# Local attention and a two-level mixture of experts: the gathered rows turned by DMA instead of on TensorE, and layer 1 in four PSUM tiles of their own

## The chip, the cores and the metric

The kernel runs on one core of a Trainium2 chip. The metric is the device time of one execution in microseconds. Before the change it is 672.78 us, the median of 3 runs (669.76, 672.78 and 676.31).

## What is computed

Attention over 8 batches, 8 heads, 576 positions and 64 channels; the first four heads look back over a window of 32 positions, the others over 32 positions four apart. Its output, 4608 rows of 512, goes through a mixture of experts: each row picks one of 4 groups and one of the 4 experts in it, and gets that expert's two-layer network, weighted by both probabilities.

```python
scores = np.where(masks[None, :, :, :], scale * np.matmul(q, k.transpose(0, 1, 3, 2)), -1000000000.0)
attn = softmax(scores)                      # max, exp, sum + 1e-09
x = np.matmul(attn, v)                      # as 4608 rows of 512
g_idx = np.argmax(x @ w_group, axis=1)      # g_w: softmax at g_idx
e_idx = np.argmax(xg @ w_expert[g], axis=1) # e_w: softmax at e_idx
h = np.maximum(xg[mask_e] @ w1[g, e], 0.0)  # 512 -> 1024
out[tok_idx] = (g_w * e_w)[:, None] * (h @ w2[g, e])   # 1024 -> 512
```

## The kernel before

The first part (the loop at L875) is the attention, tile by tile, with the routing of finished rows woven in. The attention's rows are stored to DRAM (`xd`, L350). Its product with v goes to PSUM tiles `o` in the pool psA (L303).

The second part, from about 255 us on, runs the experts in an order by size. `PIECES` (L42) holds 16 pieces, one for each expert, of 152 to 368 rows; 256-row and 128-row parts of the two largest experts are done earlier (`early`, L863) while the attention ends. For piece i, `begin(i)` (L1030) selects the row numbers on DVE, lets POOL gather the rows from DRAM (`fetch_rows`, L688: two indirect DMAs of half a row for each tile of up to 128 rows, into `xr`), and makes the tiles `xh` and `xl`, which hold the rows turned, channels on partitions, as the high and the low half in fp16. All arithmetic of the two layers is done with such pairs: high x high, low x high, high x low, three matmuls for each product.

`spread` (L713) turns the rows. For each tile of rows PE transposes four blocks of 128 x 128 fp32 into the PSUM tile `pt` (L721), ACT copies `pt` to `xh` in fp16 (L722), and DVE subtracts for `xl` (L723).

`layer1` (L736) makes the 1024 hidden channels in 8 groups of 128, numbered 0 to 7 here: 12 matmuls into one PSUM tile of 512 columns (L743), then ACT's Relu to `hh` (L750) and DVE's `hl` (L751). The PSUM tile comes from `new_a` (L729): in turn one half of the tile `second`, which lies in psA's two banks, and a tile `a` of the pool psS, which has two.

`layer2` (L759) takes the row tiles one by one: 24 matmuls each into `y` (L802; 8 hidden groups, each with hh, hl, hh), ACT's scaled copy to `yr` (L776), and POOL's scatter to the output (L763). A last tile with at most 64 rows is packed 2 or 4 times side by side; its row numbers and weights are turned by small matmuls `rp` after group 3 of layer 1 (L664 to L669: `entq` on DVE, `csq` on ACT). In the middle and at the end of each row tile `layer2` calls `between`, and this is where the next piece's rows are spread (L1071).

The weights come as 8 chunks of 512 KB per expert, issued by SP (L611) into 7 buffers. Each chunk is split by ACT into the high half (L625: wa1h, wb2h and so on) and by DVE into the low half (L622); DVE's split frees the buffer, and the next fetch is issued after it. The main loop (L1076) spreads these splits over the steps of the piece: four or five in layer 1, the rest in layer 2. `overflow` (L955), small DVE steps for rows beyond an expert's share, fills steps that have none.

The order on every engine is the order of the program from L1057 on (`manual_schedule`); an engine stops at the first instruction whose input is not there. A DMA on SP stops SP in the same way.

Of the kernel before, what the change touches and what calls it, by code (L numbers as in the profile page):

```python
# [8 lines left out]
F32 = mybir.dt.float32  # L9
F16 = mybir.dt.float16  # L10
# [3 lines left out]
ALU = mybir.AluOpType  # L14
AX = mybir.AxisListType
PSUM = bass.MemoryType.PSUM

P = 128
B, H, S, D = 8, 8, 576, 64
NTOK = B * S  # L20
DM = 512
# [21 lines left out]
CMAX = max(n for _, _, n in PIECES)  # L43
# [21 lines left out]
def moe_attention_kernel(ctx, tc, q, k, v, cmask, wgate, wpack, out):  # L65
    nc = tc.nc
    pool = lambda name, bufs=1, **kw: ctx.enter_context(tc.tile_pool(name=name, bufs=bufs, **kw))
    cp = pool("cp")
    dram = pool("dram", space=bass.MemoryType.DRAM)
    psS = pool("psS", 2, space=PSUM)  # L70
    psT = pool("psT", 2, space=PSUM)
    psA = pool("psA", 1, space=PSUM)
    psX = pool("psX", 1, space=PSUM)
    psR = pool("psR", 1, space=PSUM)

# [19 lines left out]

    att = ExitStack()
    apool = lambda name, bufs=1, **kw: att.enter_context(tc.tile_pool(name=name, bufs=bufs, **kw))
    vp = apool("vp", NV)
    qp = apool("qp", NQ)
    kr = apool("kp").tile([P, 2, 2 * NK, 8, 32], F32, name="kr")  # L100
# [121 lines left out]
    def run(gens, n=1):  # L222
        got = None
        for _ in range(n):
            while gens:
                try:
                    got = next(gens[0])
                    break
                except StopIteration:
                    gens.pop(0)  # L230
            else:
                return None
        return got
# [454 lines left out]
    def fetch_rows(xr, ent, t, known=NTOK + 1):  # L688
        for h in range(2):
            nc.gpsimd.indirect_dma_start(  # L690
                out=xr[:, 256 * h : 256 * h + 256],
                out_offset=None,
                in_=xd[0:known].rearrange("n (h c) -> (n h) c", h=2),
                in_offset=bass.IndirectOffsetOnAxis(ap=ent[:, 1 + h, t : t + 1], axis=0),
                bounds_check=2 * known - 1,
                oob_is_err=False,
            )

    def tiles(cap):
        return [(t, min(P, cap - t * P)) for t in range((cap + P - 1) // P)]  # L700

    def gather(ent, cap):
        xrs = []
        for t, n in tiles(cap):
            xr = rows.tile([P, 512], F32, name="xr", bufs=4)
            fetch_rows(xr, ent, t)
            xrs.append(xr)
        return xrs

    def new_x(pl, cap=CMAX):  # L710
        return pl.tile([P, 4, cap], F16, name="xh"), pl.tile([P, 4, cap], F16, name="xl")

    def spread(xs, xrs, cap, sel=None):  # L713
        xh, xl = xs
        for t, n in tiles(cap):
            if sel is not None and t not in sel:
                continue
            xr = xrs[t]
            pt = psT.tile([P, 4, P], F32, name="pt", tag="t")
            for c in range(4):  # L720
                nc.tensor.transpose(pt[:, c, 0:n], xr[0:n, c * P : c * P + P], id32[0:n, 0:n])  # L721
            nc.scalar.copy(xh[:, :, t * P : t * P + n], pt[:, :, 0:n])  # L722
            nc.vector.tensor_tensor(  # L723
                xl[:, :, t * P : t * P + n], pt[:, :, 0:n], xh[:, :, t * P : t * P + n], ALU.subtract
            )

    more_a = []

    def new_a():  # L729
        if more_a:  # L730
            more_a.append(more_a.pop(0))
            if more_a[0] is not None:
                return more_a[0]
        return psS.tile([P, 512], F32, name="a", tag="s")

    def layer1(w, xs, cap, new_h):  # L736
        xh, xl = xs
        hh, hl = hs[:] = new_h()
        for f in range(8):
            a = new_a()  # L740
            mm = [(ww, xx, c) for c in range(4) for ww, xx in ((w[0], xh), (w[0], xl), (w[1], xh))]
            for i, (ww, xx, c) in enumerate(mm):
                nc.tensor.matmul(  # L743
                    a[:, 0:cap],
                    ww[:, c * FF + f * P : c * FF + f * P + P],
                    xx[:, c, 0:cap],
                    start=(i == 0),
                    stop=(i == len(mm) - 1),
                )
            nc.scalar.activation(hh[:, f, 0:cap], a[:, 0:cap], AF.Relu)  # L750
            nc.vector.scalar_tensor_tensor(  # L751
                hl[:, f, 0:cap], a[:, 0:cap], 0.0, hh[:, f, 0:cap], ALU.max, ALU.subtract
            )
            yield
# [120 lines left out]
    for s in range(NT + 3):  # L875
# [12 lines left out]
        if start:  # L888
            n = start.pop()
# [23 lines left out]
        if s == NT - 1:  # L913
            room = fe.tile([P, 48 * P], F16, name="room")
            cut = lambda a, c: room[:, a * P : (a + c) * P].rearrange("p (c n) -> p c n", c=c)
            for i in range(2):
                xs, hs_ = (cut(24 * i, 4), cut(24 * i + 4, 4)), (cut(24 * i + 8, 8), cut(24 * i + 16, 8))
# [15 lines left out]
    fx = pool("fx", 2, reuse_waits="tile")  # L933
    fh = pool("fh", 2, reuse_waits="tile")
    rows = pool("rows", 2, reuse_waits="tile")
# [3 lines left out]
    def new_h():  # L939
        return fh.tile([P, 8, CMAX], F16, name="hh"), fh.tile([P, 8, CMAX], F16, name="hl")  # L940

    second = psA.tile([P, 2, 512], F32, name="second", tag="o")
    more_a[:] = [None, second[:, 0], None, second[:, 1]]
    spare = xT[NBP - 1].rearrange("p c b i -> p (c b i)")
    taken = [0]

# [79 lines left out]
    nt = lambda c: (c + P - 1) // P  # L1026

    pieces = PIECES

    def begin(i):  # L1030
        r, off, cap = pieces[i]
        ent, cs = new_slots()
        three = select(ent, cs, top[:, r] if r < NEARLY else perm[:, r], off // P, nt(cap))
        tq = note_tail(cs, three, cap)
        return ent, cs, gather(ent, cap), new_x(fx), tq

    cur = []

    def first(k):
        if 0 < k <= nt(pieces[0][2]):  # L1040
            spread(cur[3], cur[2], pieces[0][2], (k - 1,))

    def ready():
        cur[:] = begin(0)
# [18 lines left out]
    for i, (r, off, cap) in enumerate(pieces):  # L1063
        more = i + 1 < len(pieces)
        if more:
            nxt = begin(i + 1)
            ncap = pieces[i + 1][2]
            nc.gpsimd.drain()
        nsel = nt(cap)

        def between(k):  # L1071
            m, d = nt(ncap), 2 * nsel - 2
            if more and k < d:
                spread(nxt[3], nxt[2], ncap, range(m * k // d, m * (k + 1) // d))

        for k, _ in enumerate(ffn(wsets[r % 2], cur[3], cur[0], cur[1], cap, new_h, between, cur[4])):  # L1076
            k0, steps = (0, 8) if k < 8 else (8, 2 * nsel)
            if k == 0:
                todo = ahead
            elif k == 8:  # L1080
                ahead = split(r + 2, wsets[r % 2]) if r + 2 < NE else []
                todo, ahead = ahead[: NW // 2], ahead[NW // 2 :]
            if k == k0:
                chunks = len(todo)
            if (k - k0 + 1) * chunks // steps > (k - k0) * chunks // steps:
                todo.pop(0)()
            elif r > NEARLY:
                run(bgq)
        if more:
            cur = nxt  # L1090
# [3 lines left out]
    with tc.For_i(0, nov, 1) as i:  # L1094
# [13 lines left out]
        ent, cs = new_slots()  # L1108
        unpack(ent, cs, three.unsqueeze(2))
        xs = new_x(fx)  # L1110
        xr = gather(ent, P)
# [73 lines left out]
```

## Time and profile before

| | |
|---|---|
| median of 3 runs | 672.78 us |
| the profiled execution | 663.49 us, span 661.7 us, mean granted clock 0.959 |
| PE, DVE, ACT, POOL busy | 588.1, 405.4, 331.6, 249.2 us |
| hardware DMA queue | 105.31 MB |
| gathers and scatters (software DMA queue) | 20.98 MB |

The profile is of one execution. Busy time of PE is the time in which at least one matmul is under way; matmuls overlap, so a count times a mean is more than the busy time. PEld is the load of the stationary operand, which runs beside matmuls. An idle time is put down to the engine and line that ended it. The chain of work that ended last goes back from the last instruction, at each step to what released it. Times in the timeline count from the span's start.

### The profile page before, as it was taken

To read this page: it belongs to the slowest core of one execution; us is meant where nothing else is said; L and a number is where in the kernel's file an instruction comes from. 1 tells how busy PE (TensorE), PEld (TensorE's weight loads), DVE (VectorE), ACT (ScalarE), POOL (GpSimd) and SP (SyncE) were. 2 spreads that over 40 slices of the span, in tenths; PEclk is the share of its full clock that TensorE was granted. 3 is DMA by queue.
4 is the path that set the end of the run, shared out by engine and by line. 5 is a ranking of instruction groups with operands and counts; after the bars stand their busy time and mean duration, and the time that the engine had idled before them with its cause. 6 is when DMAs were issued, how large, how long until landed. Compare 5 with 4: busy or idle time off the path is not lost.

```text
span 661.7 us, 18758 instructions
## 1 busy us (share of the span) xinstructions
PE 588.1 (89%) x7636; PEld 407.9 (62%) x7636; DVE 405.4 (61%) x849; ACT 331.6 (50%) x662; POOL 249.2 (38%) x304
## 2 busy tenths in 40 slices
PE   5898799878577999879989899898999999999896
PEld 4666576556464677655556566555576577667764
DVE  6765875887834672457485777554556567575720
ACT  2455565665532643456354455454557556556521
POOL 5874554539040171415142333414154134213311
PEclk9899989898796999979999999999999999999999
DMA  7887867796551026557565656656585677678300
GB/s 260 277 280 232 258 199 224 244 333 225 164 183 37 25 72 238 192 162 245 162 189 194 181 181 207 195 163 208 157 267 193 193 259 226 236 234 266 94 27 28
DMA packets 47916, 127.53 MB, mean 193 GB/s; under 512 B 7224, under 2 KB 8126, under 8 KB 47826
## 3 DMA queue, kind: packets, MB, share of 16 engines
q1 hardware_dynamic: 40466, 105.31, 50.0%
q0 software_dynamic: 7360, 20.98, 9.3%
q8 instruction: 62, 1.02, 0.6%
q14 instruction: 28, 0.23, 0.1%
HBM read 107.38 MB, written 19.24 MB: 191 GB/s over the span
## 4 chain that ended last, share of the span: by engine, by line
PE 57%; DVE 5%; issue 5%; ACT 3%; another core or an unknown queue 1%; POOL 0%; POOLq 0%; ACTq 0%
PE y L802 29%; PE second L743 12%; PE a L743 11%; PE pt L721 3%; DVE hl L751 1%; ACT hh L750 1%; PE lg_ps L389 1%; ACT wa1h L625 1%; ACT wa2h L625 1%; DVE wb1l L622 1%; PE lt_ps L378 0%; DVE wa1l L622 0%; DVE mv L492 0%; ACT wb2h L625 0%
## 5 line engine op out<-in xcount | busy, mean ns | idle before, releaser
L690 POOL DMA_INDIRECT xr<-xd,sent x80 | 96.5, 1206 | 33.2 <-issue 22.2
L763 POOL DMA_INDIRECT out<-yr,sent x30 | 30.0, 1001 | 204.6 <-ACT yr L776 180.8
L802 PEld LDWEIGHTS <-hh 128*128 128x128 f16 (+10 forms) x960 | 67.8, 99 | 59.8 <-issue 4.8
L743 PEld LDWEIGHTS <-wa1h 128*128 128x128 f16 x640 | 59.3, 98 | 25.7 <-issue 14.2
L723 DVE TENSOR_TENSOR xl<-pt,xh 128x512 f16<-128x512 f32 (+10 forms) x42 | 24.8, 595 | 77.7 <-ACT xh L722 69.0
L743 PEld LDWEIGHTS <-wb1h 128*128 128x128 f16 x576 | 55.9, 100 | 24.0 <-issue 13.2
L776 ACT ACTIVATE yr<-y,cs 128x512 f32<-128x512 f32 (+3 forms) x30 | 20.6, 688 | 91.7 <-PE y L802 67.4
L751 DVE SCALAR_TENSOR_TENSOR hl<-second,hh 128x256 f16<-128x256 f32 (+11 forms) x68 | 29.0, 427 | 55.6 <-ACT hh L750 41.4
L802 PE MATMUL y<-wb2h,hh 128*128 128x512 f16 (+6 forms) x272 | 60.6, 307 | 0.5 <-issue 0.5
L802 PE MATMUL y<-wb2h,hl 128*128 128x512 f16 (+6 forms) x272 | 60.4, 305 | 0.3
L802 PE MATMUL y<-wb2l,hh 128*128 128x512 f16 (+6 forms) x272 | 60.2, 305 | 0.5 <-issue 0.5
L802 PE MATMUL y<-wa2h,hl 128*128 128x512 f16 (+7 forms) x208 | 56.8, 330 | 0.1
L802 PE MATMUL y<-wa2h,hh 128*128 128x512 f16 (+7 forms) x208 | 56.9, 331 | 0.0
L127 POOL TENSOR_SCALAR vs<-vt 32x520 f32<-32x520 f32 x72 | 47.9, 665 | 23.8 <-DMA vt<-v 13.0
L802 PE MATMUL y<-wa2l,hh 128*128 128x512 f16 (+7 forms) x208 | 56.7, 330 | 0.0
L131 POOL TENSOR_SCALAR vs<-vt 32x520 f32<-32x520 f32 x64 | 41.9, 654 | 35.9 <-PE o L309 32.7
L802 PEld LDWEIGHTS <-hl 128*128 128x128 f16 (+10 forms) x480 | 35.0, 100 | 26.3 <-issue 1.2
L743 PE MATMUL second<-xh,wb1h 128*128 128x256 f16 (+6 forms) x144 | 39.6, 277 | 12.1 <-DVE hl L751 11.0
L750 ACT ACTIVATE hh<-a 128x256 f16<-128x256 f32 (+11 forms) x68 | 26.3, 387 | 42.9 <-PE a L743 22.0
L751 DVE SCALAR_TENSOR_TENSOR hl<-a,hh 128x256 f16<-128x256 f32 (+11 forms) x68 | 28.9, 425 | 30.1 <-ACT hh L750 19.2
L274 PE MATMUL s<-kr,qb 128*32 128x128 f32 x1152 | 43.3, 294 | 4.5 <-DMA kr<-k 2.2
L274 PEld LDWEIGHTS s<-kr,qb 128*32 128x32 f32 x1152 | 32.5, 117 | 18.0 <-issue 13.8
(201 smaller groups left out, 1552.5 us busy)
## 6 DMA issues: line engine op xcount, KB each, us to landing
w<-wpack SPq DMA_DIRECT2D x128, 512.0 KB
vt<-v SPq DMA_DIRECT2D x36, 260.0 KB
qb<-q SPq DMA_DIRECT2D x36, 256.0 KB
xd<-x SPq DMA_DIRECT2D x72, 128.0 KB
kr<-k SPq DMA_DIRECT2D x34, 256.0 KB
xr<-xd,sent POOLq DMA_INDIRECT x80
kr<-k SPq DMA_DIRECT2D x4, 128.0 KB
out<-yr,sent POOLq DMA_INDIRECT x30
```

Of the source, the lines that this page charges most:

```text
L127: nc.gpsimd.tensor_scalar(vs[n][even], vt[n][even], 1.0, 1.0, ALU.mult, ALU.mult)
L131: nc.gpsimd.tensor_scalar(vs[n][odd], vt[n - 1][odd], 1.0, 1.0, ALU.mult, ALU.mult)
L274: nc.tensor.matmul(s[32 * j : 32 * j + 32, c].rearrange("p w k -> p (w k)"), qv[:, (sl * 2 + a) * 32 : (sl * 2 + a) * 32 + 32], kr[:, :, k ...
L690: nc.gpsimd.indirect_dma_start(out=xr[:, 256 * h : 256 * h + 256], out_offset=None, in_=xd[0:known].rearrange("n (h c) -> (n h) c", h=2), ...
L721: nc.tensor.transpose(pt[:, c, 0:n], xr[0:n, c * P : c * P + P], id32[0:n, 0:n])
L723: nc.vector.tensor_tensor(xl[:, :, t * P : t * P + n], pt[:, :, 0:n], xh[:, :, t * P : t * P + n], ALU.subtract)
L743: nc.tensor.matmul(a[:, 0:cap], ww[:, c * FF + f * P : c * FF + f * P + P], xx[:, c, 0:cap], start=(i == 0), stop=(i == len(mm) - 1),)
L750: nc.scalar.activation(hh[:, f, 0:cap], a[:, 0:cap], AF.Relu)
L751: nc.vector.scalar_tensor_tensor(hl[:, f, 0:cap], a[:, 0:cap], 0.0, hh[:, f, 0:cap], ALU.max, ALU.subtract)
L763: ins = nc.gpsimd.indirect_dma_start(out=out.rearrange("n (g c) -> (n g) c", g=g), out_offset=bass.IndirectOffsetOnAxis(ap=at, axis=0), in ...
L776: nc.scalar.activation(yr[0:n, :], yp[0:n, :], AF.Copy, scale=cs[0:n, t : t + 1])
L802: nc.tensor.matmul(yp[P // g * j : P // g * j + n, 0 : DM // g], h[:, f, t * P : t * P + n], ww[:, f * DM + DM // g * j : f * DM + DM // g ...
```

## The change

The rows are turned without PE. For each gathered tile, ACT copies the 128 x 512 fp32 rows to fp16 into the left half of a tile `both`, DVE writes the rest, rows minus that copy, into the right half, and SP issues one DMA transpose of `both` (up to 128 rows x 1024) into the piece's tile `xx` (128 partitions x 8 blocks x rows), of which `xh` is the first four blocks and `xl` the others. The number of rows turned is rounded up to 16. One tile is turned for each step of the generator `turning`; the steps are taken after groups 4 and 6 of layer 1 and then at layer 2's calls of `between`. `spread` remains for the early pieces and the overflow. There are 3 buffers for `xr` and not 4.

In layer 1 the tile `second` goes; psA's banks are given back after the attention and a pool psB with two tiles takes their place, so that the 8 groups go in turn to four tiles of one bank each.

```diff
-    psA = pool("psA", 1, space=PSUM)
...
+    psA = apool("psA", 1, space=PSUM)
...
     def gather(ent, cap):
...
-            xr = rows.tile([P, 512], F32, name="xr", bufs=4)
+            xr = rows.tile([P, 512], F32, name="xr", bufs=3)
...
-    def new_x(pl, cap=CMAX):
-        return pl.tile([P, 4, cap], F16, name="xh"), pl.tile([P, 4, cap], F16, name="xl")
+    def new_x(pl):
+        xx = pl.tile([P, 8, CMAX], F16, name="xx")
+        return xx[:, 0:4], xx[:, 4:8], xx
+
+    def turning(xs, xrs, cap):
+        for t, n in tiles(cap):
+            both = rows.tile([P, 2 * DM], F16, name="both", bufs=3)
+            nc.scalar.copy(both[:, 0:DM], xrs[t])
+            nc.vector.tensor_tensor(both[:, DM : 2 * DM], xrs[t], both[:, 0:DM], ALU.subtract)
+            n = (n + 15) // 16 * 16
+            nc.sync.dma_start(xs[2][:, :, t * P : t * P + n], both[0:n], transpose=True)
+            yield
...
-    more_a = []
+    more_a = [psS]
 
     def new_a():
-        if more_a:
-            more_a.append(more_a.pop(0))
-            if more_a[0] is not None:
-                return more_a[0]
-        return psS.tile([P, 512], F32, name="a", tag="s")
+        more_a.append(more_a.pop(0))
+        return more_a[0].tile([P, 512], F32, name="a", tag="s")
...
-    second = psA.tile([P, 2, 512], F32, name="second", tag="o")
-    more_a[:] = [None, second[:, 0], None, second[:, 1]]
+    more_a[:] = [psS, pool("psB", 2, space=PSUM, reuse_waits="tile")]
...
-        return ent, cs, gather(ent, cap), new_x(fx), tq
+        xrs, xs = gather(ent, cap), new_x(fx)
+        return ent, cs, xrs, xs, tq, [turning(xs, xrs, cap)]
...
     def first(k):
-        if 0 < k <= nt(pieces[0][2]):
-            spread(cur[3], cur[2], pieces[0][2], (k - 1,))
+        run(cur[5])
...
         def between(k):
-            m, d = nt(ncap), 2 * nsel - 2
-            if more and k < d:
-                spread(nxt[3], nxt[2], ncap, range(m * k // d, m * (k + 1) // d))
+            if more:
+                run(nxt[5])
...
+            if k in (4, 6):
+                between(k)
```

Three places in the piece of 288 rows show how the instructions stand. Line numbers of the rows after the change are those of the changed file (L750 is the matmul of layer 1 there, L757 `hh`, L717 and L718 the two halves of `both`, L720 the DMA transpose).

First, PE in layer 1, at a group that waits for DVE. Before, this is the third group, number 2:

```order
L743 LDWEIGHTS wb1l
L743 MATMUL a<-xh,wb1l 128x288
L743 LDWEIGHTS wb1h
L743 MATMUL second<-xh,wb1h 128x288 [waits DVE_49]
L743 LDWEIGHTS wb1h
L743 MATMUL second<-xl,wb1h 128x288
```

And with the change the fifth, number 4, right behind the small matmuls `rp` of the tail:

```order
L666 MATMUL rp<-tq,id_73 32x2 [waits PE_49]
L666 MATMUL rp<-tq,id_73 32x2 x3
L750 LDWEIGHTS wb1h
L750 MATMUL a<-xx,wb1h 128x288 [waits DVE_49]
L750 LDWEIGHTS wb1h
L750 MATMUL a<-xx,wb1h 128x288
```

Groups 2, 4 and 6 waited for DVE before; now groups 4 to 7 do.

Second, ACT in the same layer 1, from the second pair of groups on (`wa2h` is the split of a weight chunk for a later piece). Before:

```order
L625 ACTIVATE wa2h<-w_6807 128x1024
L750 ACTIVATE hh<-second 128x288
L750 ACTIVATE hh<-a 128x288
L669 COPY csq<-rp 128x1
L625 ACTIVATE wa2h<-w_6840 128x1024
L750 ACTIVATE hh<-second 128x288
L625 ACTIVATE wa2h<-w_6859 128x1024
L750 ACTIVATE hh<-a 128x288
L750 ACTIVATE hh<-second 128x288
L625 ACTIVATE wa2h<-w_6932 128x1024
L750 ACTIVATE hh<-a 128x288
L776 ACTIVATE yr<-y,cs 128x512
```

With the change:

```order
L625 ACTIVATE wa2h<-w_6784 128x1024
L757 ACTIVATE hh<-a 128x288 x2
L669 COPY csq<-rp 128x1
L625 ACTIVATE wa2h<-w_6822 128x1024
L757 ACTIVATE hh<-a 128x288
L717 CAST both<-xr 128x512
L625 ACTIVATE wa2h<-w_6841 128x1024
L757 ACTIVATE hh<-a 128x288 x2
L717 CAST both<-xr 128x512
L625 ACTIVATE wa2h<-w_6904 128x1024
L757 ACTIVATE hh<-a 128x288
L717 CAST both<-xr 128x512
```

The three copies of gathered rows stand behind groups 4, 6 and 7; before, the three copies `xh` stood among layer 2's `yr`. DVE's subtracts stand at the same places on DVE.

Third, SP over the same stretch, where the rows before were weight fetches alone (the ISA row sets the address of a fetch):

```order
L611 DMA w_6761<-wpack 128x1024
L720 DMA_TRANSPOSE xx<-both 128x8x128
L611 ISA
L611 DMA w_6784<-wpack 128x1024
L720 DMA_TRANSPOSE xx<-both 128x8x128
L611 ISA
L611 DMA w_6822<-wpack 128x1024
L611 ISA
L611 DMA w_6841<-wpack 128x1024
L720 DMA_TRANSPOSE xx<-both 128x8x32
L611 ISA
L611 DMA w_6904<-wpack 128x1024
```

Three DMA transposes have come in between the fetches of the piece; each waits for DVE's subtract, and the fetches below it wait behind it.

More of the change, by code (lines that the diff above doesn't have):

```diff
@@ L708, in gather @@
         return xrs
-    def new_x(pl, cap=CMAX):
-        return pl.tile([P, 4, cap], F16, name="xh"), pl.tile([P, 4, cap], F16, name="xl")
+    def new_x(pl):
[9 more added lines that the diff above has]
+            yield
     def spread(xs, xrs, cap, sel=None):
-        xh, xl = xs
+        xh, xl = xs[0:2]
         for t, n in tiles(cap):
@@ L725, in spread @@
             )
-    more_a = []
+    more_a = [psS]
     def new_a():
-        if more_a:
-            more_a.append(more_a.pop(0))
-            if more_a[0] is not None:
-                return more_a[0]
-        return psS.tile([P, 512], F32, name="a", tag="s")
+        more_a.append(more_a.pop(0))
+        return more_a[0].tile([P, 512], F32, name="a", tag="s")
     def layer1(w, xs, cap, new_h):
-        xh, xl = xs
+        xh, xl = xs[0:2]
         hh, hl = hs[:] = new_h()
@@ L1066, in moe_attention_kernel @@
             nxt = begin(i + 1)
-            ncap = pieces[i + 1][2]
             nc.gpsimd.drain()
```

## The prediction

> **What bounds the kernel now.** I read first the page's busy times, then the busy time piece by piece through the expert stage, then the chain of work that ended last, then who waited for whom, and last single stretches of the timeline. The stage that the change touches runs from about 255 us to the end.
>
> ```profile
> PE 588.1 (89%) x7636; PEld 407.9 (62%) x7636; DVE 405.4 (61%) x849; ACT 331.6 (50%) x662; POOL 249.2 (38%) x304
> 330.00:360.00 30.00, 27.40 (x209) 17.64 (x208) 20.67 (x53) 14.58 (x24) 9.52 (x9) 1.00 0.59 180
> 551.50:573.30 21.80, 21.80 (x154) 15.09 (x153) 14.36 (x24) 12.90 (x20) 6.91 (x6) 1.00 0.74 244
> 573.30:594.00 20.70, 20.70 (x150) 15.34 (x148) 13.42 (x23) 12.73 (x20) 6.81 (x6) 1.00 0.76 243
> by line: PE y L802 29.2%; PE second L743 12.5%; PE a L743 11.1%; issue 4.6%; PE pt L721 2.8%; DVE hl L751 1.2%; another core or an unknown queue 0.9%; ACT hh L750 0.7%; PE lg_ps L389 0.6%; ACT wa1h L625 0.6%; ACT wa2h L625 0.6%; DVE wb1l L6
> ```
>
> The three window rows give, in this order, the stretch, its length, then busy time of PE, PEld, DVE, ACT and POOL with instruction counts, the granted clock, the DMA share and GB/s. In a piece of two row tiles (551.5 to 573.3) PE is busy for the whole stretch; DVE has 7 us to spare, ACT 9 us, and the DMA engines a quarter. In a piece of three tiles (330 to 360) PE lacks 2.6 us of being full. So PE sets the pace, and time leaves the kernel in two ways only: less PE work, or fewer PE gaps. The chain says the same: y, second and a are the two layers, and the transposes of the gathered rows (pt, L721) are 2.8% of 661.7, or 18.5 us.
>
> **The transposes that PE loses.** What one tile costs PE is seen in the chain between two runs of layer 2's matmuls, and in the rows of the instructions themselves.
>
> ```profile
> 346.03 5.18 PE y L802 x24
> 351.64 1.42 PE y L802 x24
> 353.65 1.42 PE y L802 x24
> 355.46 5.29 PE y L802 x24
> 540.40 2.59 PE y L802 x12
> 543.42 2.59 PE y L802 x12
> 546.45 5.18 PE y L802 x24
> L721 PE MATMUL pt<-id,xr 128*128 128x128 f32 (+10 forms) x160 | 22.4, 262 | 0.0
> ```
>
> 346.03 + 5.18 ends at 351.21 and the next run starts at 351.64: 0.43 us for four transposes. The next two seams are 0.59 and 0.39 (the last for 48 rows); in the two-tile piece 0.43 and 0.44. 160 transposes are 40 tiles, 16 pieces: eight of three tiles at 1.41 us and eight of two at 0.87 make 11.3 + 7.0 = 18.3 us. That agrees with the chain's 18.5 us (part of which is the early pieces' transposes, which stay), and the 22.4 us of busy time is more because it overlaps matmuls. I take **-18 us**. Bounds: -16 if the seams keep 0.05 us each, -22 if all of the busy time goes.
>
> **The waits for `second`.** The next rows are one line of the waits, six of the timeline in the piece of 152 rows, four of the chain and one window.
>
> ```profile
> PE second L743 <- DVE hl L751: 18.9, 11, 4.8
> 273.06 0.23 PE L743 MATMUL second<-xh,wb1h 128*128 128x152 f16 x1
> 273.85 0.23 PE L743 MATMUL a<-xh,wb1h 128*128 128x152 f16 x1
> 275.11 0.32 DVE L751 SCALAR_TENSOR_TENSOR hl<-second,hh 128x152 f16<-128x152 f32 x1 [1.49 <-ACT hh L750]
> 275.48 0.23 PE L743 MATMUL second<-xh,wb1h 128*128 128x152 f16 x1 [0.68 <-issue]
> ...
> 284.60 0.32 DVE L751 SCALAR_TENSOR_TENSOR hl<-second,hh 128x152 f16<-128x152 f32 x1 [1.96 <-ACT hh L750]
> 284.97 0.28 PE L743 MATMUL second<-xh,wb1h 128*128 128x152 f16 x1 [4.81 <-DVE hl L751]
> 273.22 0.79 PE second L743 x12
> 284.97 1.68 PE second L743 x12
> 448.68 1.47 PE second L743 x12
> 461.09 3.04 PE second L743 x12
> 448.00:479.00 31.00, 27.61 (x263) 17.54 (x261) 14.56 (x23) 14.81 (x26) 9.06 (x9) 0.94 0.58 179
> ```
>
> Group 0 of this layer 1 writes one half of `second` at 273.06, group 1 a tile of psS at 273.85, group 2 the other half at 275.48. Group 2 needs nothing that group 0 holds, but it starts 0.05 us after DVE has read group 0's half (275.11 + 0.32 = 275.43). So the two halves are guarded as one tile: every even group waits for the even group before it, two back, while the odd ones go four back. All 11 waits, 18.9 us, are on `second`; none of length is on `a`. With four tiles of their own, each group waits for the one four back. The long waits come at group 6, for group 4, when a weight split or the tail's small copies hold ACT and DVE up; group 2, which group 6 would wait for now, is long done. But the late results are only put off: layer 2 wants the last hh and hl near the end of its first tile, so part may come back there. I take **-14 us** (bounds 0 and -18.9).
>
> After the 4.81 us wait, the same 12 matmuls took 1.68 us where they took 0.79; after the wait at 461, 3.04 where 1.47: the granted clock drops for a while behind a long gap (0.94 in the window from 448 to 479, 1.00 in those quoted before). These two cost about 0.9 + 1.6 us in the first group and as much again behind it, some 4 us. I take **-3 us**, with bounds 0 and -4.
>
> **What is added on ACT and DVE.** Per tile, a copy to fp16 and a subtract replace the two evictions of pt, now from SBUF and always 512 wide.
>
> ```profile
> L625 ACT ACTIVATE wa1h<-w 128x1024 f16<-128x1024 f32 x32 | 33.6, 1059 | 0.1
> L622 DVE SCALAR_TENSOR_TENSOR wb2l<-w,wb2h 128x1024 f16<-128x1024 f32 x32 | 38.9, 1216 | 0.0
> L723 DVE TENSOR_TENSOR xl<-pt,xh 128x512 f16<-128x512 f32 (+10 forms) x42 | 24.8, 595 | 77.7 <-ACT xh L722 69.0 <-ACT yr L776 8.7
> L751 DVE SCALAR_TENSOR_TENSOR hl<-second,hh 128x256 f16<-128x256 f32 (+11 forms) x68 | 29.0, 427 | 55.6 <-ACT hh L750 41.4 <-ACT wa1h L625 5.4 <-ACT yr L776 3.2
> 529.58 1.31 PE second L743 x12
> 531.86 1.05 POOL L690 DMA_INDIRECT xr<-xd,sent  x1 [0.30 <-issue]
> 536.70 1.00 POOL L690 DMA_INDIRECT xr<-xd,sent  x1 [0.30 <-issue]
> ```
>
> Half of a weight split's 1059 and 1216 ns is 0.53 and 0.61 us: the same work as before, hidden beside PE. What differs is the place: layer 1, behind groups 4 and 6, where ACT and DVE now stop in order until the gathered rows have landed, with the weight splits and the last hh and hl queued behind them, which PE waits for in layer 2. In the piece that starts at 529.58, the fourth gather's issue ends at 537.70; group 6 is due on ACT at 529.58 + 7 x 1.31 = 538.75. If the rows land 3 us after issue, ACT stands 2 us, and copy (0.53), subtract (0.61), split (1.22) and the last hl (0.43) end at about 543.5. Layer 2 starts at 540.06 and asks for that hl in the last 3 of its 24 matmuls (5.18 us), at 544.6. So 1 us is to spare; if they land 6 us after issue, 2 us are missing. No row shows the landing. Bounds 0 and +30 us (2 us in 15 pieces); I take **+4 us**, near the lower, because in three-tile pieces the groups are longer and the margin larger.
>
> **The 40 DMA transposes.** No row shows one. Nearest rows:
>
> ```profile
> q1 hardware_dynamic: 40466, 105.31, 50.0%
> q0 software_dynamic: 7360, 20.98, 9.3%
> SPq L611 <- DVE wa1l L622: 81.3, 15, 12.6
> SPq L611 <- DVE wb1l L622: 69.4, 15, 7.8
> SPq L611 <- DVE wa2l L622: 53.5, 27, 5.7
> ```
>
> By bytes: the hardware queue's 105.31 MB took 50% of the span, 331 us, or 3.14 us per MB of all 16 engines; a tile of 128 x 1024 fp16 is 0.262 MB, 0.82 us. By packets: the gather's queue spent 9.3% of 661.7 us on 7360 packets, 0.134 us of one engine each; were each of the tile's 1024 runs of 256 bytes a packet, a tile would take 1024 x 0.134 / 16 = 8.6 us. I take 1.6 us, nearer the first end: a tile is read in whole 2 KB rows, and two stages with different mixes (0.59 at 180 GB/s, 0.74 at 244 GB/s) both pay 3.0 to 3.3 us per MB. The free share is (1 - 0.59) x 30 = 12.3 us for three tiles, or (1 - 0.74) x 21.8 = 5.7 us for two; so at 1.6 us the transposes fit and cost **0**. Their cover is layer 2: the last of them is issued at its start, and 10 to 13 us pass before the next piece's first matmul, which waits for it. If that cover goes, each us late is 1 us per piece. On SP a transpose waits for DVE's subtract with the next weight fetches behind it. But the fetches wait for DVE's splits anyway, 204 us in the three rows quoted, and a fetch runs nearly a piece ahead of its use; SP has several us per transpose to give.
>
> A page of the Trainium skill speaks against the change: "VectorE: DVE Perf Modes", section "The three transpose paths", gives 390 ns for a 128 x 128 transpose on TensorE and 1309 ns on the DMA path, and its rules for kernel authors prefer TensorE where the result may go to PSUM. Eight such blocks in a row would be an estimated 10.5 us a tile, beside the 8.6 us above; the page "DMA: Bandwidth & Descriptors", section "Latency and other measured facts", has 261 GB/s for DMA transposes, an estimated 1.0 us a tile, beside the 0.82 us. On this trace PE pays about 110 ns per transpose at the seam. Which of the two figures holds decides between the forecast and the slow rival below; no run here shows it yet.
>
> **Sum.** -18 - 14 - 3 + 4 + 0 = -31 us against the profiled execution's 663.49 us (span 661.7): 632.5 us. The median of the three runs shown, 672.78, is 1.4% above that execution; scaled by 672.78 / 663.49 = 1.014 the forecast is **641 us**.
>
> **Rivals.**
> *Waits come back (0.11).* The late hh and hl only move PE's wait from `second` into layer 2's first tile: the 17 us of waits and clock are lost again, the transposes stay gained. For it: ACT and DVE get two or three more instructions in just that part of layer 1. Against: they have 7 us and more to spare per piece. 663.5 - 18 = 645.5, times 1.014: 655 us.
> *No net change (0.06).* The gathers land 6 us after issue and cost 2 us in every piece, +30 us: 663.5 - 35 + 30 = 658.5, or 668 us.
> *DMA binds (0.23), slower.* A transpose takes the 16 engines not 1.6 but up to 8.6 us. It decides from 12.3 / 3 = 4.1 us in three-tile pieces and 5.7 / 2 = 2.8 us in two-tile pieces; beyond that the weight chunks in the same queue fall behind and ACT waits for them. At 8.6 us a three-tile piece needs 17.7 + 25.8 = 43.5 us for 30, a two-tile piece 16.1 + 17.2 = 33.3 for 21.8: 8 x 13.5 + 6 x 11.5 = 177 us, 840 times 1.014: 852 us; near the threshold, 680. For it: 256-byte runs and no row of such a transfer. Against: the constant price per MB.
> *The change does not part the tiles*: if the new pool's tiles were guarded as one again, the waits would stay, and the time would be the first rival's.
>
> **How the numbers follow.** Forecast 0.60, rivals 0.11, 0.06, 0.23. The forecast's own range is 627 to 658 us: best ends -22 - 18.9 - 4 give 618.6 or 627, and half of the gain gives 657. The range 622 to 692 takes in the two middle cases and the edge of the slow one and leaves out most of the latter. A measurement of this kernel tells about 1% from no change. Faster by over 1%: 0.60 + 0.11 = 0.71; within 1%: 0.06; slower by over 1%: 0.23.
>
> **What would show it.** Right: no pt seams between runs of y; PE's waits for hl in layer 1 under 3 us in total; PE hardly waiting for the transposed tile at the start of layer 1; the DMA share in two-tile pieces up by 0.1 or so and PE still full. Wrong: PE waiting on a DMA at each piece's start, the share near 1 and weight splits waiting for their chunks (the slow rival); ACT idle before the copies of gathered rows by over 2 us a piece and PE gaps in layer 2's first tile (the other two).

## The result, and the profile after

The changed kernel takes 638.88 us, the median of four runs (635.74 to 644.94), beside 671.27 us (666.93 to 676.31) for the kernel before on the same chip: a ratio of 0.953, 95% interval 0.943 to 0.963. Two repeats on other chips gave 0.946 (0.940 to 0.953) and 0.949 (0.944 to 0.954). So it is faster by 4.7 to 5.4%, and the forecast, 641 us, was 2 us off. Two traces alone would mislead here: the profiled execution of before (663.49 us) lay below all of its runs, and that of after (644.94 us) was the slowest of its four, so they differ by 18.5 us where the medians differ by 32. Ratios leave disturbed executions out, in which the whole run is some per cent longer, so a ratio may differ from the quotient of two medians, most of all where the table below lists before with 678.80 us (five of its eleven runs there were such).

The page of the changed kernel, with its busy times and its two large DMA queues:

```profile
PE 574.8 (89%) x7476; PEld 394.3 (61%) x7476; DVE 406.6 (63%) x849; ACT 332.9 (52%) x662; POOL 251.5 (39%) x304
...
q1 hardware_dynamic: 75058, 113.90, 60.4%
q0 software_dynamic: 7360, 20.98, 10.4%
```

PE has 160 transposes fewer (7636 - 7476). The hardware queue has 34592 packets more, 865 on average for each of the 40 DMA transposes, 8.59 MB more (0.215 MB for the average transpose, 248 bytes a packet), and 0.604 x 643.2 - 0.500 x 661.7 = 57.6 us more of all 16 engines: 1.44 us per transpose. So the runs of 256 bytes did become packets, but cheap ones. The share adds up the times of the packets, and these can overlap (from 293.0 to 302.2 us of this trace it is 1.13), so the price is rather an upper bound.

The chain of work of the changed kernel, from a late point in the first tile of layer 2 of one three-tile piece to layer 1 of the next:

```profile
353.33 8.62 PE y L809 x74
361.96 6.20 PE a L750 x48
368.16 0.21 PE rp L666 x4
```

The three seams of 0.4 to 0.6 us between runs of y are gone. Layer 2 stops once, for 0.49 us just before 353.33, for a late `hl`; from there on it is one run, and layer 1 of the next piece follows at once. The waits, of PE, of its weight loads and of ACT, from 255 us on:

```profile
PE a L750 <- DMA xx<-both: 7.2, 3, 6.0
...
PE y L809 <- DVE hl L758: 3.5, 6, 1.1
...
PEld L809 <- DVE hl L758: 7.0, 9, 1.6
...
ACT both L717 <- DMA xr<-xd,sent: 14.1, 9, 2.7
```

The columns are the sum in us, the times and the longest. No wait of PE for `hl` inside layer 1 is left, where there were 18.9 us. In their place stand two new ones: 3.5 us for late `hl` in layer 2 (the weight load's 7.0 us lies partly beside matmuls), and 7.2 us for the turned rows, 6.0 of them in one piece, the third, of 368 rows. SP's issues of that piece's transposes, PE's first matmul behind them, and three windows (columns as in the prediction):

```profile
269.71 16.68 SPq L611 DMA_DIRECT2D w<-wpack  x5
287.78 1.27 SPq L720 DMA_TRANSPOSE xx<-both  x1
...
293.09 1.22 SPq L720 DMA_TRANSPOSE xx<-both  x1
```

```profile
302.14 0.77 PE L750 MATMUL a<-xx,wa1h 128*128 128x368 f16 x2 [5.97 <-DMA xx<-both]
```

```profile
258.00:302.00 44.00, 34.08 (x400) 24.42 (x397) 23.07 (x46) 23.38 (x44) 12.45 (x14) 0.91 0.93 249
527.00:548.00 21.00, 20.77 (x145) 13.89 (x143) 14.41 (x24) 12.80 (x20) 7.40 (x6) 1.00 0.97 277
548.00:570.00 22.00, 21.62 (x150) 14.41 (x149) 14.67 (x25) 12.67 (x20) 7.51 (x6) 1.00 0.88 263
```

From 258 to 302 us the weight chunks of the first experts catch up and the DMA engines are busy to 0.93; the third transpose is issued at 293.09 and PE gets the rows at 302.14, 9 us later. SP was not late with it, since DVE had finished the tile's half only at 292.98. The packets from 294.7 to 297.0 us, and from there to 301.6, show where the time went:

```profile
DMA packets 209, 0.80 MB, mean 347 GB/s; under 512 B 14, under 2 KB 14, under 8 KB 209
DMA packets 1016, 0.51 MB, mean 111 GB/s; under 512 B 947, under 2 KB 947, under 8 KB 1016
```

The packets of a transpose are the small ones. The issue ends at 294.31, but up to 297.0 nearly all packets are large ones, those of weight chunks; only then do the transpose's packets run, and they last 4.5 us. PE was free at 296.17, so it would have waited about 1 us even if the rows had come 2.7 us after the issue, as they do in an experiment below. In two-tile pieces the DMA share is now 0.88 to 0.97 where it was 0.74 to 0.76, and PE is still nearly full.

### The profile page after: what moved, and what is told of

It is laid out like the page before. It is cut to its first block, busy times and chain, and to the rows that moved or that the text cites. A ratio compares the mean times of both kernels' runs of the same rounds, so it can differ in the third digit from the quotient of the medians.

```text
span 643.2 us, 18563 instructions
## 1 busy us (share of the span) xinstructions
PE 574.8 (89%) x7476; PEld 394.3 (61%) x7476; DVE 406.6 (63%) x849; ACT 332.9 (52%) x662; POOL 251.5 (39%) x304
## 5 line engine op out<-in xcount | busy, mean ns | idle before, releaser
L758 DVE SCALAR_TENSOR_TENSOR hl<-a,hh 128x256 f16<-128x256 f32 (+11 forms) x136 | 56.8, 425 | 93.9 <-ACT hh L757 60.4
L770 POOL DMA_INDIRECT out<-yr,sent x30 | 38.0, 1266 | 188.9 <-ACT yr L783 159.4
L690 POOL DMA_INDIRECT xr<-xd,sent x80 | 92.5, 1156 | 37.5 <-issue 23.5
L750 PE MATMUL a<-xx,wb1h 128*128 128x256 f16 (+6 forms) x576 | 95.3, 272 | 4.0 <-issue 3.4
L750 PE MATMUL a<-xx,wa1h 128*128 128x192 f16 (+7 forms) x512 | 91.0, 282 | 7.1 <-DMA xx<-both 6.5
L757 ACT ACTIVATE hh<-a 128x256 f16<-128x256 f32 (+11 forms) x136 | 50.8, 385 | 68.2 <-PE a L750 51.1
L750 PE MATMUL a<-xx,wb1l 128*128 128x256 f16 (+6 forms) x288 | 77.8, 272 | 1.8 <-issue 1.8
L750 PEld LDWEIGHTS <-wa1h 128*128 128x128 f16 x640 | 60.0, 99 | 22.7 <-issue 12.5
L750 PE MATMUL a<-xx,wa1l 128*128 128x192 f16 (+7 forms) x256 | 72.2, 282 | 0.4 <-issue 0.3
L750 PEld LDWEIGHTS <-wb1h 128*128 128x128 f16 x576 | 54.8, 99 | 15.2 <-issue 4.3
L131 POOL TENSOR_SCALAR vs<-vt 32x520 f32<-32x520 f32 x64 | 40.4, 632 | 42.0 <-PE o L309 39.0
L127 POOL TENSOR_SCALAR vs<-vt 32x520 f32<-32x520 f32 x72 | 48.0, 666 | 22.1 <-DMA vt<-v 11.9
```

The lines of the kernel that those rows point to most:

```text
L127: nc.gpsimd.tensor_scalar(vs[n][even], vt[n][even], 1.0, 1.0, ALU.mult, ALU.mult)
L131: nc.gpsimd.tensor_scalar(vs[n][odd], vt[n - 1][odd], 1.0, 1.0, ALU.mult, ALU.mult)
L690: nc.gpsimd.indirect_dma_start(out=xr[:, 256 * h : 256 * h + 256], out_offset=None, in_=xd[0:known].rearrange("n (h c) -> (n h) c", h=2), ...
L750: nc.tensor.matmul(a[:, 0:cap], ww[:, c * FF + f * P : c * FF + f * P + P], xx[:, c, 0:cap], start=(i == 0), stop=(i == len(mm) - 1),)
L758: nc.vector.scalar_tensor_tensor(hl[:, f, 0:cap], a[:, 0:cap], 0.0, hh[:, f, 0:cap], ALU.max, ALU.subtract)
L770: ins = nc.gpsimd.indirect_dma_start(out=out.rearrange("n (g c) -> (n g) c", g=g), out_offset=bass.IndirectOffsetOnAxis(ap=at, axis=0), in ...
```

## The experiments

Kernels of one group ran on the same chip, beside runs of the kernel before. All times are medians in us.

| run | time (range) | before there | ratio to before, 95% |
|---|---|---|---|
| DMA transposes alone | 653.67 (650.73-658.51) | 671.57 | 0.973 (0.969-0.978) |
| four tiles alone | 647.55 (643.74-648.66) | 671.57 | 0.963 (0.959-0.967) |
| each transpose twice | 648.03 (644.39-652.83) | 671.57 | 0.966 (0.961-0.970) |
| all turning in layer 2 | 642.26 (639.49-647.24) | 671.57 | 0.958 (0.953-0.962) |
| the change again | 636.92 (633.99-637.82) | 678.80 | 0.946 (0.940-0.953) |
| third piece on PE | 630.22 (625.79-632.82) | 678.80 | 0.937 (0.930-0.944) |
| steps behind 5 and 7 | 634.14 (631.07-636.59) | 678.80 | 0.944 (0.938-0.950) |
| both of these | 633.04 (630.38-635.12) | 678.80 | 0.941 (0.935-0.947) |
| before again, one run | 636.86 | 633.89 | |
| ACT issues the transposes | 659.34 (652.76-663.73) | 633.89 | 1.046 (1.041-1.051) |
| before, rp later | 670.52 (667.32-675.41) | 671.10 | 1.001 (0.997-1.004) |
| the change, third time | 637.02 (632.06-639.05) | 671.10 | 0.949 (0.944-0.954) |

### The two parts apart

The DMA transposes alone: the changed kernel, with layer 1's tiles as before.

```diff
-    more_a[:] = [psS, pool("psB", 2, space=PSUM, reuse_waits="tile")]
+    second = psA.tile([P, 2, 512], F32, name="second", tag="o")
+    more_a[:] = [None, second[:, 0], None, second[:, 1]]
```

> The rows are turned by DMA as in the change, but layer 1 keeps the tile `second` in two halves. My theory: the transposes' 18 us leave PE, 4 us come back as the stop for gathered rows, and the waits of PE for `second` inside layer 1 stay near 19 us: 657 us beside a before of 671 (ratio 0.979, 0.970 to 0.988). Rival A, the tiles were worth nothing because the late hl only moved to layer 2: 639 us (0.952), the whole gain. Rival B, the transposes only trade PE work for DMA waits and the whole gain is the tiles': 668 to 675 us (0.995 to 1.005).

The four tiles alone: the kernel before, with

```diff
-    second = psA.tile([P, 2, 512], F32, name="second", tag="o")
-    more_a[:] = [None, second[:, 0], None, second[:, 1]]
+    more_a[:] = [psS, pool("psB", 2, space=PSUM, reuse_waits="tile")]
```

(with `new_a` and the place of psA as in the change).

> Four tiles of their own in layer 1, rows still turned on PE. My theory: 14 us of waits and 3 us of clock leave, 18 us of pt in the chain stay: 654 us beside 671 (ratio 0.975, 0.965 to 0.985), with PE's waits for hl in layer 1 under 3 us and some 4 us of waits for hh and hl in layer 2. Rival A (waits come back in layer 2's first tile): 668 to 671 us (0.995 to 1.0). Rival B (the whole gain is the tiles'): 639 us (0.952). Together with the run of the DMA transposes alone this shows whether the two parts add: 18 - 4 and 14 + 3 would make 31 us.

Alone, the transposes give 17.9 us, inside the theory's range, and the tiles 24.0 us, just beyond the theory's range (a ratio of 0.963 where it ended at 0.965) and short of rival B. PE's first waits from 255 us on, of the transposes alone and of the tiles alone:

```profile
PE second L753 <- DVE hl L761: 22.7, 10, 4.7
PE y L812 <- DVE hl L761: 1.0, 2, 0.5
PE second L753 <- DMA xx<-both: 1.0, 1, 1.0
```

```profile
PE a L740 <- issue: 7.1, 13, 1.0
```

With the old tiles the waits for `second` are all there. With the new tiles PE has no wait for hl or hh, neither in layer 1 nor in layer 2. (A row with "issue" says that PE waited for nothing that the profile shows.) Rival A of the second run, that the waits come back in layer 2, has fallen. The late results themselves have not gone. Here is ACT's hh of group 3 in the piece of 288 rows, with the tiles alone:

```profile
447.59 0.41 ACT L747 ACTIVATE hh<-a 128x288 f16<-128x288 f32 x1 [3.19 <-PE a L740]
```

ACT gets PE's result as late as with the old tiles, and PE goes on, because it has more free tiles to write to.

The two gains do not add up: 17.9 + 24.0 = 41.9, and the change gives 34.1 on the chip of its third run (671.10 - 637.02). Some 8 us are lost between the parts; by the ratios of the three groups and their intervals it may be several us more or less. The transposes alone show only 1.0 us of waiting for `xx`, where the change has 7.2: beside the waits for `second` the late rows hardly show.

### The change again

The same kernel, in the group of the next two experiments.

> The change itself once more, beside the variants that build on it. Every theory expects 639 us beside a before of 671 (ratio 0.952, 0.945 to 0.960); it also tells whether 32 us is what the two parts give together, where 18 (DMA transposes alone) and 24 (tiles alone) would make 42.

636.92 us; PE's wait for the third piece's rows is 3.34 us in this trace, where it was 5.97. In the trace of the third time it is 7.54.

### What a transpose costs

```diff
             nc.sync.dma_start(xs[2][:, :, t * P : t * P + n], both[0:n], transpose=True)
+            spot = room[:, t * 8 * P : t * 8 * P + 8 * P].rearrange("p (c n) -> p c n", c=8)
+            nc.sync.dma_start(spot[:, :, 0:n], both[0:n], transpose=True)
```

> As the change, but each of the 40 DMA transposes is issued twice, the second into a region that nothing reads (the output is the same). It prices a transpose. My theory: one takes 1.4 us of the 16 engines (the queue's share goes from 60 to about 69%); three-tile pieces have the room, two-tile pieces (DMA share 0.9 in the trace of the change) do not, so 2 us or less come in each of some seven pieces and 4 us at the first pieces: 650 us where the change has 639 (ratio to before 0.968, 0.955 to 0.985). Rival A, the DMA engines have room everywhere: 639 to 642 us (0.952 to 0.957). Rival B, the transposes stand on the path already, each second one adds its 1.4 us: 695 us (1.036); if they are 2.5 us on SP and the fetches behind them are late too, more.

648.03 us, 9 to 11 us above the change's 637 to 639 (on other chips), as the theory had it. Forty more transposes add 0.23 to 0.28 us each. The queue and PE's wait, with the transposes doubled:

```profile
q1 hardware_dynamic: 109650, 122.49, 66.8%
```

```profile
PE a L752 <- DMA xx<-both: 13.6, 6, 7.5
```

0.668 x 646.8 is 432.1 us of the queue, where the change again has 0.599 x 635.9 = 380.9: 51 us more, or 1.28 us per transpose. PE's wait for turned rows goes to 13.6 us, 7.5 of them in the third piece; another 3.1 us are put down to a doubled transpose. The theory had the time right, but the place only in part: beside 4 us at the first pieces it saw seven two-tile pieces short of room, and all these waits but one of 1.6 us lie in pieces of three tiles. So a transpose is mostly hidden, and what shows of it is the late rows.

### Who should issue them

```diff
-            nc.sync.dma_start(xs[2][:, :, t * P : t * P + n], both[0:n], transpose=True)
+            nc.scalar.dma_start(xs[2][:, :, t * P : t * P + n], both[0:n], transpose=True)
```

> As the change, but ACT issues the DMA transposes and not SP, so they do not stand behind weight fetches in SP's queue, and their descriptors do not stand in one ring with the weight chunks. My theory of the late rows of the third piece (368 rows): the transposes wait in the ring behind up to seven weight chunks that are catching up; then PE's wait for `xx` there (3.3 to 6.0 us) falls under 1 us. ACT pays for it: it stops for DVE's subtract (0.69 us) and the issue (1.2 us) 40 times, so some hl come late in layer 2: 634 to 642 us in all (ratio 0.943 to 0.955 by the chip's before). Rival, the 16 engines are simply full there (0.93): the wait for `xx` stays at 3 us or more.

659.34 us, slower than any theory had it, on a chip where the kernel before takes 633.89 us. The change itself was not run there, but it never took over 645 us elsewhere. One of its pieces on ACT, its queues, the longest wait of PE in layer 2 and one of ACT's:

```profile
411.12 0.62 ACT L717 CAST both<-xr 128x512 f16<-128x512 f32 x1
412.49 1.26 ACTq L720 DMA_TRANSPOSE xx<-both  x1
413.79 1.06 ACT L625 ACTIVATE wb2h<-w 128x1024 f16<-128x1024 f32 x1 [2.06 <-DVE wb2l L622]
```

```profile
q1 hardware_dynamic: 40466, 105.31, 51.7%
...
q10 hardware_dynamic: 34592, 8.59, 10.5%
```

```profile
PE y L809 <- ACT hh L757: 25.9, 15, 2.9
```

```profile
ACT wb2h L625 <- DVE wb2l L622: 30.8, 14, 3.3
```

ACT stops from the end of its copy, 411.74, to 413.79 in the first tile shown, and about as long in the others: first for DVE's half of `both`, then for the issue, which ends at 413.75. (The profile puts this idle time down to DVE's weight split, which ran meanwhile.) The `hh` queued behind come late, and PE waits 25.9 us for them in layer 2. On SP the same stop holds up only weight fetches that have time: in the trace of the change neither ACT nor DVE waits for a weight chunk. PE's wait for `xx` was 2.4 us here, neither under 1 nor over 3; all of it is in the third piece:

```profile
278.50 1.25 ACTq L720 DMA_TRANSPOSE xx<-both  x1
282.94 0.77 PE L750 MATMUL a<-xx,wa1h 128*128 128x368 f16 x2 [2.37 <-DMA xx<-both]
```

PE has the rows 3.2 us after the end of the issue (279.75 to 282.94), where the change needed 7.8 us (294.31 to 302.14). So the 2.4 us come from a late issue, and the further delay of the change is not there. That would fit the order in the ring, but the DMA share at that point was 0.78 (278.5 to 283.0) and not 1.13 (293.0 to 302.2), so this run does not tell the order in the ring from the share of the engines.

It does price a transpose by itself, since the 40 have a queue of their own: 0.105 x 651.0 / 40 = 1.71 us of the 16 engines. On the page "VectorE: DVE Perf Modes" of the Trainium skill, section "The three transpose paths", 1309 ns stand for a 128 x 128 block, and on "DMA: Bandwidth & Descriptors", section "Latency and other measured facts", 261 GB/s. For the eight blocks of a full tile these give an estimated 10.5 and 1.0 us. The 1.28 to 1.71 us measured are for the average transpose of 0.215 MB (126 to 168 GB/s), or 1.6 to 2.1 us for a full tile of 0.262 MB: much nearer to the second.

### When the rows are turned

```diff
-            if k in (4, 6):
-                between(k)
```

> As the change, but without the turning steps after groups 4 and 6 of layer 1: all gathered rows are turned at layer 2's steps. My theory: ACT's 14 us of waits for gathered rows go to zero and so do PE's waits for hl in layer 2 (7 us), but in pieces of two tiles the last transpose is issued 5 us before the end of layer 2 and lands about 1 us late, in three-tile pieces it is just in time: 639 to 650 us (ratio 0.952 to 0.968), PE's waits for the turned tile 10 us or more in sum. Rival, the stop in layer 1 is what costs and the transposes are early anyway: 630 us (0.939). Rival, the transposes need the early start by 3 us and more a piece: 680 us (1.013).

642.26 us, inside the theory's range. PE's wait for the turned rows, and one two-tile piece:

```profile
PE a L750 <- DMA xx<-both: 16.1, 10, 8.1
```

```profile
522.54 5.26 SPq L720 DMA_TRANSPOSE xx<-both  x2
```

```profile
530.49 0.38 PE L750 MATMUL a<-xx,wb1h 128*128 128x256 f16 x2 [1.02 <-DMA xx<-both]
```

The second issue ends at 527.80 and PE has the rows at 530.49, 2.7 us later. Waiting for `hl` in layer 2 is gone, but 16.1 us of waiting for rows have come, half of it in the third piece. The early start is worth what the stop in layer 1 costs, or a little more (ratios 0.958 and 0.946 to 0.953, on different chips).

The steps one group later, `if k in (5, 7)`:

> As the change, but the two turning steps of layer 1 stand behind groups 5 and 7 and not 4 and 6. My theory: the rows are there one group (1.3 us) later, so ACT's waits for them fall from 14 us to some 4, PE's waits for hl in layer 2 from 10 us of weight load and matmul to 3, and no transpose comes later than PE needs it: 634 us (ratio 0.945). Rival, the transposes land late instead (as when all of them stood in layer 2): 640 to 643 us (0.953 to 0.958), with more PE waits for `xx`.

634.14 us, the number expected, and one half of the reason given. ACT's waits for gathered rows did not fall: they are 13.0 us in its trace, where the change again has 11.8. The waits for `hl` in layer 2, of PE and of its weight loads, did: 0.9 us, where the change again has 4.5. Its range touches that of the change again (633.99 to 637.82), so whether it is faster stays open.

### The third piece on PE

```diff
+ON_PE = (2,)
...
+    def by_pe(xs, xrs, cap):
+        for t, n in tiles(cap):
+            spread(xs, xrs, cap, (t,))
+            yield
...
-        return ent, cs, xrs, xs, tq, [turning(xs, xrs, cap)]
+        return ent, cs, xrs, xs, tq, [(by_pe if i in ON_PE else turning)(xs, xrs, cap)]
...
-            if k in (4, 6):
+            if k in (4, 6) and i + 1 not in ON_PE:
```

> As the change, but the rows of the piece of 368 rows (the third, turned while the weight chunks catch up and the DMA share is 0.93) are turned on PE as before, in layer 2's steps; all other pieces by DMA. My theory of the 9 us that the transposes gave less than 18 on top of the tiles: two thirds of it is this one piece (6.0 us of PE waiting for `xx` and 3 us at a low clock behind it), and three seams of 0.47 us come back: 8 us less than the change, 631 us (ratio 0.940). Rival, the loss is spread over all pieces as waits for hl in layer 2 and contention: 638 to 640 us (0.950 to 0.954). Rival, the late weight chunks of this stretch hold PE up anyway, by another wait: 639.

630.22 us: 6.7 us below the change on the same chip, and the two ranges do not meet. PE's waits from 255 us on, and the stretch in which the weights catch up:

```profile
PE a L756 <- issue: 6.6, 12, 1.0
PE y L815 <- DVE hl L764: 1.1, 3, 0.5
PE a L756 <- DVE xx L739: 0.3, 1, 0.3
```

```profile
258.00:302.00 44.00, 39.92 (x411) 26.74 (x409) 25.67 (x47) 25.13 (x45) 14.86 (x14) 0.92 0.77 254
```

No wait of a matmul for a DMA is left, and PE is busy for 39.92 of these 44 us, not 34.08. So this one piece holds 6.7 us, most of what the two parts lose together. It is the fastest version found. With the later steps as well:

> Both edits: the piece of 368 rows turned on PE, and the steps behind groups 5 and 7. If the two losses are the ones named and independent: 8 + 5 us less than the change, 626 us (ratio 0.932, 0.925 to 0.942), and PE full to 99% from 300 us on. Rival, they are not what costs: 636 to 640 us (0.948 to 0.953).

633.04 us: no further gain, and neither the theory's 626 us nor the rival's 636 to 640. The two losses were not independent, or the second was none.

### Where the waits for `second` come from

> The kernel before, unchanged, profiled once more: the execution whose trace the prediction rests on took 663.49 us, the shortest of all runs of this kernel, and the others lie at 667 to 682. If the long executions differ in the expert stage (383 us from the first layer 1 to the last in the trace shown), PE's waits for `second` should be longer than 18.9 us here, by up to 10 us; if they differ in the attention, the stage should take 383 us again and start later than 255.7 us. Its time: 671 us.

Both expectations missed: 636.86 us, on a chip where the kernel before takes 633.89 us (629.29 to 646.10 in eleven runs). PE's wait for `second` in this trace:

```profile
PE second L743 <- DVE hl L751: 5.1, 6, 2.2
```

The expert stage, from the first layer 1 matmul of the first piece to that of the last (249.40 to 612.47), takes 363.1 us here and 383.1 us in the trace of the prediction; 13.8 of these 20 us are the waits. So the waits that the four tiles remove are no fixed property of the program. In the trace of the prediction most of them lie in pieces where ACT and DVE get PE's results 2 to 4 us late, right behind the matmuls `rp`. Hence this edit to the kernel before, which moves only these:

```diff
-            if tq is not None and f == 3:
+            if tq is not None and f == 7:
```

> The kernel before, with one thing moved: the small matmuls `rp` of the tail, and the copies entq and csq behind them, stand after group 7 of layer 1 and not after group 3. In the trace of before, five of the eleven waits for `second`, 15.8 of 18.9 us, come right behind pieces in which entq on DVE starts 3 to 4.5 us after rp on PE; in the trace of 635 us it starts 0.7 to 1.5 us after it in all pieces but one and the waits are 5.1 us. My theory: these late results are what the tile `second` turns into PE waits, and four tiles bridge. Then here the waits for `second` fall to 5 us or less, the late results are met by layer 2's first tile (5.2 us long) and mostly hidden, and the time is 14 to 18 us below before (ratio 0.974 to 0.979, where before is at 670). Rival, the waits come from the weight splits in ACT's and DVE's order and not from rp: 668 to 672 us (0.995 to 1.0). On a chip where before takes 634 us: no difference above 4 us.

670.52 us, no difference, and the theory falls: the late results stay where they were, with `rp` gone from there. PE's waits, and ACT in the piece of 288 rows:

```profile
PE second L743 <- DVE hl L751: 21.8, 11, 4.1
```

```profile
454.49 0.41 ACT L750 ACTIVATE hh<-second 128x288 f16<-128x288 f32 x1 [0.22 <-PE second L743]
458.09 0.41 ACT L750 ACTIVATE hh<-a 128x288 f16<-128x288 f32 x1 [3.19 <-PE second L743]
```

Here hh of group 3 starts 3.6 us after that of group 2, where PE's groups take 1.5 us. The time is that of the rival, the weight splits in ACT's and DVE's order, but its reason does not fit this row: ACT's split before it ended at 454.28 (453.23 + 1.05), and ACT then stood idle. No run moved the splits. What makes the results late is left open; the last section has what stands beside it.

> The change once more, on whatever chip this is. Where before takes 670 us, 637 to 639 (ratio 0.946 to 0.953). Where before takes 634 us, as in the last runs, only the transposes can be gained, since its waits for `second` are 5 us and not 19: 634 - 18 - 4 + 4 for the third piece and the late hl = 616 us (ratio 0.972, 0.965 to 0.985). Rival: there the change gains as much as elsewhere, 602 us (0.95), or nothing, 634.

637.02 us beside 671.10: the first case. How much the change gains on the chip where before takes 634 us was not tried.

## Why the prediction was right, point by point

**PE sets the pace; the transposes are worth 18 us.** PE's part is right: no seam is left. With the stop for gathered rows the sum had -18 + 4 = -14 us, and alone the transposes gave 17.9 (14.7 to 21.0 by the interval of the ratio), so the stop hardly shows, or the transposes are worth more than 18.

**The waits for `second`, 14 + 3 us.** That the two halves were guarded as one was right, and four tiles removed the waits. The reason given for the late results, that a weight split or the tail's small copies hold ACT and DVE up, was not borne out: ACT stands idle before the late hh, and moving `rp` with its copies changed nothing. The size was too small: alone the tiles gave 24.0 us. First, I kept back 5 us for results that come late again in layer 2, and the tiles alone show no such wait. Second, the trace I worked from was a good execution. The first layer 1 matmul of the first piece and of the last, in before (663.49 us), in the run with `rp` moved, which takes as long as before (670.55 us profiled), and in the tiles alone:

```profile
255.73 0.25 PE L743 MATMUL second<-xh,wa1h 128*128 128x192 f16 x1
638.86 0.25 PE L743 MATMUL second<-xh,wb1h 128*128 128x192 f16 x1
```

```profile
253.61 0.25 PE L743 MATMUL second<-xh,wa1h 128*128 128x192 f16 x1
646.00 0.25 PE L743 MATMUL second<-xh,wb1h 128*128 128x192 f16 x1
```

```profile
256.36 0.25 PE L740 MATMUL a<-xh,wa1h 128*128 128x192 f16 x1
624.29 0.25 PE L740 MATMUL a<-xh,wb1h 128*128 128x192 f16 x1
```

That is 383.1, 392.4 and 367.9 us. Against the trace shown the tiles save 15.2 us, near the 17 of the sum; against the longer execution 24.5, as the medians have it. The 8 us between the profiled execution and the median lay in the stage of the change, at least in part in the very waits; I spread them over the whole kernel with the factor 1.014, which gave 0.2 us to these terms. (This holds as far as the run with `rp` moved stands for before.)

**ACT and DVE stop for gathered rows, +4.** Near: ACT waited 14.1 us, PE 3.5 us in layer 2 in the trace of after, and 0.8 in that of the change again. The copy takes 0.61 us and the subtract 0.69, each 0.08 more than I took from half a split.

**The DMA transposes, 1.6 us each and nothing on the path.** The price was right, at its low end: by three ways a full tile takes 1.6 to 2.1 us. That nothing of it lies on the path was the step that failed, by 7 us. I weighed their share against the room in pieces in full swing, and there they do fit, though only just (0.88 to 0.97). I did not weigh the stretch from 258 to 302 us, where the weights catch up; there the rows of the third piece are issued late and land late, and PE waits for them. Two of the signs I named came out otherwise: PE does wait at the start of layer 1 (7.2 us), and the DMA share in two-tile pieces rose by 0.12 to 0.23 and not by 0.1 or so.

**The sum.** Measured: -17.9 (the stop in it) - 24.0 + 7.8 (lost between the parts) = -34.1. The forecast's -18 - 17 + 4 + 0 = -31 came out near it by luck: the gain of the tiles was put 7 us too low, that of the transposes with their stop 4 us too low, and the 8 us that the two lose together at nothing. The errors cancelled.

**Rivals.** "Waits come back" and "no net change" have fallen with the tiles alone and with the waits after. "DMA binds" has fallen at 1.44 us against thresholds of 4.1 and 2.8 (its 177 us counted six of the eight two-tile pieces). The tiles are parted.

## What to carry to other kernels

Weigh an added transfer against the fullest stretch that it passes through, at the start of a stage above all, and not against the steady pieces; one piece out of sixteen held most of its cost, and leaving that piece on the old path was worth another 7 us. An in-order engine that must wait for another's half result should be one with nothing urgent behind it: on SP the stops for the 40 transposes held up nothing that was waited for, on ACT they delayed hh. A wait that looks like a property of the program can be one execution's: look at several before pricing it, and value deeper buffering by what it bridges.

## What the runs showed of the hardware that was not expected

The late results coincide with POOL's gathers of a certain length. POOL's first and last gather of six, and ACT's late hh, in the piece of 288 rows in before; then the last gathers and hh of the same group on the chip where before takes 634 us:

```profile
450.97 1.05 POOL L690 DMA_INDIRECT xr<-xd,sent  x1 [0.30 <-issue]
...
457.55 1.00 POOL L690 DMA_INDIRECT xr<-xd,sent  x1 [0.30 <-issue]
```

```profile
456.78 0.41 ACT L750 ACTIVATE hh<-a 128x288 f16<-128x288 f32 x1 [2.48 <-PE second L743]
```

```profile
433.66 1.05 POOL L690 DMA_INDIRECT xr<-xd,sent  x1 [0.30 <-issue]
...
438.94 1.32 POOL L690 DMA_INDIRECT xr<-xd,sent  x1 [0.30 <-issue]
440.57 1.64 POOL L690 DMA_INDIRECT xr<-xd,sent  x1 [0.30 <-issue]
```

```profile
437.29 0.41 ACT L750 ACTIVATE hh<-a 128x288 f16<-128x288 f32 x1 [1.06 <-PE a L743]
```

In before the six gathers take 7.6 us (450.97 to 458.55) and ACT gets group 3's result some 2 us late; there they take 8.5 us (433.66 to 442.21), the last two being longer, and ACT is on time. The last five pieces of before that have six gathers fall alike: where the six take 7.6 or 7.7 us (three pieces), ACT stands idle for 2.5 to 3.2 us before a hh; where they take 9.5 or 9.6 us (two), for no more than 1.6. In the traces of the tiles alone, of `rp` moved and of the change the third time, ten of the eleven sets of six gathers that take 7.6 or 7.7 us stand beside such an idle time of 2.5 us or more, and none of the eight longer ones beside more than 1.8. Either POOL's gathers are held up or the other engines' results are. This is a coincidence in the traces; no run varied the gathers, and its cause stays open.
